# Attention over channels and a highway layer on one Trainium2 core: the instruction order from a planner with priorities replaced by a list of 1,492 tasks, and the softmax chain cut into single steps

## The chip, the cores and the metric

The kernel runs on one core of one Trainium2 chip. The metric is the device time of one execution in microseconds (us). The engines are TensorE (PE, its weight loads PEld), VectorE (DVE), ScalarE (ACT), GpSimd (POOL) and SyncE (SP). GpSimd and SyncE issue the DMA transfers here, GpSimd the loads, which turn float32 into float16 on their way, and SyncE the stores.

## What is computed

For each of four batches q, k and v have 6336 rows of 256 channels. The columns of q and k are divided by their norms over the rows, a 256 x 256 matrix of their products goes through a softmax, and v times that matrix passes through a highway layer:

```python
qn = q / (np.linalg.norm(q, axis=1, keepdims=True) + 1e-06)
kn = k / (np.linalg.norm(k, axis=1, keepdims=True) + 1e-06)
s = kn.transpose(0, 2, 1) @ qn / tau
a = np.exp(s - s.max(-1, keepdims=True))
a /= a.sum(-1, keepdims=True) + 1e-09
x = v @ a                          # for each batch, then all rows together
H = np.maximum(x @ w_h, 0.0)
T = 1.0 / (1.0 + np.exp(-(x @ w_t + b_t)))
out = T * H + (1.0 - T) * x
```

The output has 25344 rows of 256 in float32. tau is 1.

## The kernel before, in words

**Tiles.** A batch is read in six chunks of eight row blocks (128 rows by 256 channels each; a chunk of q, k or v is 1 MiB of float32) and a tail of two blocks of 96 rows. The first batch's last chunks and the second batch's first are loaded in parts. The pools hold five chunks each of q, k and v, and seven of the output (`o`).

**Stage one** (`stage1`, L440) takes the 50 row blocks of a batch one after the other and accumulates, for each half of k's channels, k'q (L452), k'k (L453) and q'q (L455) in two PSUM banks. In batches 1 to 3 the q'q matmul is left out for the first five chunks; instead ScalarE squares q (L470) and GpSimd adds the squares up (`sum_squares`, L472 to L487), and three small matmuls and copies (L516, L522) turn the sum over partitions.

**The chain** (`plan_chain`, L537) follows the last block of a batch: VectorE takes the diagonals (L569) and adds the sums (L606), GpSimd takes their square root as a power (L580), VectorE takes reciprocals (L586, L589) and spreads those of q over two diagonal matrices (L594), TensorE makes a row of them for all partitions (L628), VectorE scales the copied products (L620 copies, L634 scales), ScalarE takes exponentials (L643), TensorE transposes them (L677), the transposed blocks are copied (L533 or L535), and TensorE multiplies them by both weight matrices (L689). What results, `mr`, holds for each half of the channels the softmax itself times -0.5 (L663), and its products with w_h and w_t (L700, L702).

**Stage two** takes two row blocks of v at a time, a group; there are 25 in a batch and 100 in all, numbered g. TensorE transposes v (L760, in the last batch L754; its chunks 3 to 6 are transposed by a DMA, L768), the result is copied to SBUF (L533, L535), and three products of four matmuls follow (`products`, L800): h with the first weights, t with the second, and x (the profile calls its bank d) with the softmax. The bias is copied into the bank of t beforehand (L533, L535), or from group 67 on for odd groups added by a matmul (L831), which then uses a bank that stage one has left. ScalarE makes d from h (L840) and uu from t (L854); VectorE makes pp from both (L861) and the output o from h and pp (L880).

**What sets the order.** Every piece is a `Task` (L64) with an engine, a key (its group number plus an entry of `PRIO`, L31), two durations and what it depends on. `Plan.run` (L115) simulates the engines and the DMA queues with these numbers, at each moment picks for a free engine the ready task with the lowest key, and lets ACT or DVE take a copy, whichever is free. What comes out is the order in which the instructions are written; at run time each engine works through its own queue in that order, waiting on semaphores. Loads keep an order of their own (L421), and between the last steps of a batch's stage one and the power for k no load is issued (`loads_stop`, L615). The plan lets at most eight loads be under way.

**Stores** go out on SyncE. A store of a chunk would compete with loads; so `plan_holds` (L921) puts a small DMA before it, a hold, that reads one row of the output chunk five later (`LAG`) and so makes SyncE wait until this chunk has been begun.

Of the kernel before, what the change touches and what calls it, by code (L numbers as in the profile page):

```python
# [15 lines left out]
P = 128  # L16
# [6 lines left out]
AHEAD = 16  # L23
BY_DMA = 3
SHORT = 1.08
MOVE = 165e3
APART = 5
V_AHEAD = 2


PRIO = {  # L31
    "tr": (24.974, 16.445, 34.195, 63.304),
    "ev": (74.59, 73.008, 67.512, 50.704),
    "h": (-53.39, -86.015, -64.208, -14.641),
    "bias": (-28.394, 23.065, -1.772, 4.453),
    "t": (4.111, -1.918, 67.766, 74.312),
    "relu": (46.555, -20.175, -1.498, 14.915),
    "x": (0.958, -19.433, 43.343, -6.4),
    "gate": (-54.132, 37.28, -94.231, -112.222),
    "prod": (-40.861, -10.819, -26.763, -55.482),  # L40
    "res": (53.604, 18.42, 116.457, -9.113),
    "s1": (117.419, 42.459, 84.45),
    "sq": (-15.195, 72.384, 19.395),
}
POW = 0.75
HEAD = 5.5
TAIL = 66
EV = BIAS = ("ACT", "DVE")
ENDS = [18, 48.5, 62.25]


class Ring:


    def __init__(self, bufs):
        self.bufs = bufs
        self.freed = []

    def open_at(self, t):
        n = len(self.freed) - self.bufs  # L60
        return n < 0 or (self.freed[n] is not None and self.freed[n] <= t)


class Task:  # L64
# [3 lines left out]

    def __init__(self, eng, key, pitch, lat, deps, fn, take=(), drop=(), size=0, follows=()):
        self.eng, self.key, self.pitch, self.lat = eng, key, pitch, lat
        self.deps, self.fn, self.take, self.drop, self.size = deps, fn, take, drop, size
        self.follows = follows
        self.start = self.done = None
        self.late = 0.0
        self.soft = 0
        self.held = {}
        self.serial = False

    def engines(self):
        return self.eng if isinstance(self.eng, tuple) else (self.eng,)

    def settle(self, e):
        n = self.eng.index(e)
        self.pitch, self.lat = self.pitch[n], self.lat[n]
        self.fn = partial(self.fn, e)
        self.eng = e


class Plan:

# [8 lines left out]
    def __init__(self):  # L101
        self.tasks = []
        self.rings = {}

        self.loads_stop, self.sums_stop = [], []

    def ring(self, tag, bufs):
        self.rings[tag] = Ring(bufs)

    def add(self, *args, **kw):  # L110
        t = Task(*args, **kw)
        self.tasks.append(t)
        return t

    def run(self):  # L115
        queues = {"POOL": [], "SP": []}
        in_order = {"POOL": [], "SP": []}
        users, followers = {}, {}
        for n, x in enumerate(self.tasks):
            x.n, x.left, x.at = n, len(x.deps) + len(x.follows), 0.0  # L120
            for d in x.deps:
                users.setdefault(d, []).append(x)
            for d in x.follows:
                followers.setdefault(d, []).append(x)
            if x.size or x.serial:
                in_order[x.eng].append(x)
        for lst in in_order.values():
            lst.sort(key=lambda x: (x.key, x.n), reverse=True)
        engines = list(dict.fromkeys(x.eng for x in self.tasks if not isinstance(x.eng, tuple)))
        avail = {e: [x for x in self.tasks if e in x.engines() and not x.left and not (x.size or x.serial)] for e in engines}  # L130
        free = dict.fromkeys(engines, 2.1)
        lanes, order, events = [], [], [0.0, 2.1]
        t, left = 0.0, len(self.tasks)
        eps = 1e-6

        def ready(x):
            return (
                not x.left
                and x.at <= t + eps
                and all(self.rings[g].open_at(t + eps) for g in x.take)  # L140
                and (x.eng != "POOL" or not x.size or sum(d > t + eps for d in lanes) < self.LANES)
            )

        def finish(x, when):
            x.done = when
            events.append(when)
            for owner, tag in x.drop:
                self.rings[tag].freed[owner.held[tag]] = when
            release(users.get(x, ()), when)

        def release(us, when):
            for u in us:
                u.left -= 1
                u.at = max(u.at, when)
                if not u.left and not (u.size or u.serial):
                    for e in u.engines():
                        avail[e].append(u)

        def pick(e):
            quiet = held(self.sums_stop)  # L160
            best = min(
                (x for x in avail[e] if ready(x) and not (quiet and x.soft >= quiet)),
# [3 lines left out]
            if best is None and lst and ready(lst[-1]) and not (e == "POOL" and held(self.loads_stop)):  # L166
                return lst[-1]
# [61 lines left out]
def kernel(  # L229
# [192 lines left out]
    def natural(b):  # L422

        return b == B - 1
# [670 lines left out]
```

## Time and profile before

| | |
|---|---|
| median of three runs | 270.29 us (270.16 to 270.86) |
| span of the profiled execution | 268.3 us |
| its own time outside the span | not given; the median is 2.0 us above the span |
| TensorE, matmuls busy | 246.4 us (92%) |
| ScalarE busy | 195.1 us (73%) |
| VectorE busy | 181.6 us (68%) |
| GpSimd busy | 131.7 us (49%) |
| written by DMA | 67.24 MB |
| memory read and written | 78.38 MB and 25.95 MB |
| first matmul begins; last four matmuls (0.44 us) begin | 8.95 us; 262.04 us |

The profile is one execution seen by the hardware profiler. "Busy" is the share in which an engine had an instruction under way; ends of matmuls are modelled, so that a busy TensorE may still have short holes. A DMA share can be above 1 because packets overlap. In the slices below, each digit is one fortieth of the span (6.7 us) in tenths. A line such as `45.40:95.00 49.60, 49.09 (x488) ...` gives a stretch, its length, and the busy time and instructions of each engine in it.

### The profile page before, as it was taken

To read this page: it belongs to the slowest core of one execution; us is meant where nothing else is said; L and a number is where in the kernel's file an instruction comes from. 1 tells how busy PE (TensorE), PEld (TensorE's weight loads), DVE (VectorE), ACT (ScalarE), POOL (GpSimd) and SP (SyncE) were. 2 spreads that over 40 slices of the span, in tenths; PEclk is the share of its full clock that TensorE was granted. 3 is DMA by queue.
4 is the path that set the end of the run, shared out by engine and by line. 5 is a ranking of instruction groups with operands and counts; after the bars stand their busy time and mean duration, and the time that the engine had idled before them with its cause. 6 is when DMAs were issued, how large, how long until landed. Compare 5 with 4: busy or idle time off the path is not lost.

```text
span 268.3 us, 6249 instructions
## 1 busy us (share of the span) xinstructions
PE 246.4 (92%) x2430; PEld 216.6 (81%) x2430; DVE 181.6 (68%) x377; ACT 195.1 (73%) x365; POOL 131.7 (49%) x167
## 2 busy tenths in 40 slices
PE   0697977999999999999999999999999999999991
PEld 0596864889989978999999878999998778888880
DVE  1000035777766789557878797586878998998994
ACT  1001016978888789999898887787798999998980
POOL 7233468688778064695689138567655110000000
PEclk9999999999999999999999999999999999999998
DMA  6999999999999999999999999999999999999995
GB/s 107 215 211 208 206 206 202 212 213 214 214 213 212 213 214 255 247 263 269 275 286 258 267 267 254 249 236 281 287 280 239 284 214 304 379 399 165 351 423 232
DMA packets 24622, 67.24 MB, mean 251 GB/s; under 512 B 9104, under 2 KB 11280, under 8 KB 21648
## 3 DMA queue, kind: packets, MB, share of 16 engines
q0 software_dynamic: 13472, 39.20, 75.0%
q1 hardware_dynamic: 11120, 27.64, 29.0%
q8 instruction: 19, 0.31, 0.4%
q14 instruction: 11, 0.09, 0.1%
HBM read 78.38 MB, written 25.95 MB: 389 GB/s over the span
## 4 chain that ended last, share of the span: by engine, by line
PE 76%; DMA 12%; ACT 5%; POOL 2%; issue 2%; DVE 2%; ACTq 0%; DVEq 0%; POOLq 0%
PE h L800 16%; PE t L800 16%; PE d L800 15%; PE sg L452 12%; DMA k<-in_k_dram 10%; PE sg L453 6%; PE vtps L760 5%; DMA v<-in_v_dram 2%; ACT uu L854 2%; PE sg L455 2%; PE t L831 1%; PE vtps L754 1%; PE ah L689 1%; POOL q L327 1%; ACT d L840 1%
## 5 line engine op out<-in xcount | busy, mean ns | idle before, releaser
L800 PEld LDWEIGHTS <-vtsb 128*128 128x128 f16 (+1 forms) x1044 | 98.8, 99 | 17.3 <-issue 3.2
L452 PE MATMUL sg<-q,k 128*128 128x256 f16 x384 | 83.8, 277 | 12.7 <-DMA k<-in_k_dram 12.6
L861 DVE SCALAR_TENSOR_TENSOR pp<-uu,d 128x512 f32<-128x512 f32 (+1 forms) x100 | 68.0, 684 | 28.4 <-PE d L800 16.1
L453 PE MATMUL sg<-k 128*128 128x128 f16 x384 | 76.8, 223 | 0.0
L854 ACT ACTIVATE uu<-t 128x512 f32<-128x512 f32 (+1 forms) x100 | 59.7, 597 | 19.1 <-PE t L800 18.5
L880 DVE SCALAR_TENSOR_TENSOR o<-h,pp 128x512 f32<-128x512 f32 x96 | 65.5, 686 | 1.7
L840 ACT ACTIVATE d<-h 128x512 f32<-128x512 f32 (+1 forms) x100 | 57.9, 584 | 5.7 <-PE h L800 4.9
L800 PE MATMUL t<-mr,vtsb 128*128 128x256 f16 (+1 forms) x348 | 52.2, 272 | 1.5 <-ACT t L533 1.2
L800 PE MATMUL h<-mr,vtsb 128*128 128x256 f16 (+1 forms) x348 | 51.2, 272 | 0.5 <-ACT vtsb L533 0.5
L800 PE MATMUL d<-mr,vtsb 128*128 128x256 f16 (+1 forms) x348 | 51.5, 272 | 0.1
L452 PEld LDWEIGHTS <-k 128*128 128x128 f16 x384 | 38.0, 99 | 16.7 <-DMA k<-in_k_dram 13.9
L476 POOL TENSOR_TENSOR sq<-sq,sq 128x1024 f32<-128x1024 f32 x15 | 35.4, 2361 | 16.7 <-ACT sq L470 16.6
L453 PEld LDWEIGHTS <-k 128*128 128x128 f16 x384 | 38.0, 99 | 1.5
L533 ACT COPY t<-bias_all 128x512 f32<-128x512 f32 (+1 forms) x60 | 35.4, 591 | 1.4
L455 PE MATMUL sg<-q 128*128 128x128 f16 x144 | 32.5, 226 | 0.0
L470 ACT ACTIVATE sq<-q 128x1024 f32<-128x1024 f16 x30 | 31.3, 1053 | 0.0
L760 PE MATMUL vtps<-ident,v 128*128 128x128 f32 x144 | 27.8, 275 | 0.9 <-DMA v<-in_v_dram 0.6
L569 DVE SCALAR_TENSOR_TENSOR junk<-sg,ident 128x128 f32<-128x128 f32 x16 | 4.6, 288 | 33.2 <-PE sg L455 32.7
L535 DVE COPY vtsb<-vtps 128x256 f32<-128x256 f32 (+2 forms) x47 | 19.6, 418 | 7.0 <-PE vtps L760 6.7
L327 POOL DMA_DIRECT2D v<-in_v_dram x24 | 13.7, 571 | 18.9 <-PE vtps L760 11.7
L327 POOL DMA_DIRECT2D q<-in_q_dram x28 | 15.4, 552 | 15.1 <-DMA q<-in_q_dram 7.1
L327 POOL DMA_DIRECT2D k<-in_k_dram x28 | 15.3, 548 | 13.1 <-DMA k<-in_k_dram 9.2
(78 smaller groups left out, 249.5 us busy)
## 6 DMA issues: line engine op xcount, KB each, us to landing
out_dram<-o SPq DMA_DIRECT2D x23, 1024.0 KB, 9.6
v<-in_v_dram POOLq DMA_DIRECT2D x24, 512.0 KB, 16.6
q<-in_q_dram POOLq DMA_DIRECT2D x21, 512.0 KB, 16.2
k<-in_k_dram POOLq DMA_DIRECT2D x21, 512.0 KB, 18.0
q<-in_q_dram POOLq DMA_DIRECT2D x5, 256.0 KB, 9.6
k<-in_k_dram POOLq DMA_DIRECT2D x5, 256.0 KB, 8.9
out_dram<-o SPq DMA_DIRECT2D x2, 512.0 KB, 4.2
out_dram<-ot SPq DMA_DIRECT2D x4, 192.0 KB, 5.1
```

Of the source, the lines that this page charges most:

```text
L327: nc.gpsimd.dma_start(out=t[:, s : s + n, :], in_=main_rows(src)[:, j * CH + s : j * CH + s + n, :])
L452: nc.tensor.matmul(sg[c][:, 0:C], kc, qa, start=first, stop=False)
L453: nc.tensor.matmul(sg[c][:, C : C + P], kc, kc, start=False, stop=False)
L455: nc.tensor.matmul(sg[c][:, C + P : C + 2 * P], qa[:, cs], qa[:, cs], start=False, stop=last)
L476: add(out=sq, in0=sq, in1=other)
L533: nc.scalar.copy(out=out, in_=in_)
L760: nc.tensor.transpose(ps[:, u, 0:nr], v.bitcast(f32), ident0[0:nr, 0:nr])
L800: nc.tensor.matmul(out[0:nr, u, :], vt[u][kt][:, 0:nr], mr[kt][:, col * C : (col + 1) * C], **flags(u, kt))
L840: nc.scalar.activation(out=d[0:nr, :, :], in_=ps_t["h", b, i][0:nr, :, :], func=Act.Relu, scale=0.5)
L854: nc.scalar.activation(out=uu[0:nr, :, :], in_=ps_t.pop(("t", b, i))[0:nr, :, :], func=Act.Tanh, scale=-0.5)
L861: nc.vector.scalar_tensor_tensor(out=pp[0:nr, :, :], in0=el.pop(("uu", b, i))[0:nr, :, :], scalar=1.0, in1=ps_t.pop(("d", b, i))[0:nr, :, ...
L880: nc.vector.scalar_tensor_tensor(out=ot, in0=ps_t.pop(("h", b, i))[0:nr, :, :], scalar=0.0, in1=el.pop(("pp", b, i))[0:nr, :, :], op0=AluO ...
```

## The change

`Plan.run` no longer simulates. It walks through a list `ORDER`, written out in the file, and calls the function of each task named there; after a slash stands the engine for the copies that may run on two. `L` are loads, `s1.8` step 8 of batch 1's stage one, `tr`, `ev`, `h`, `b`, `t`, `r`, `x`, `g`, `p`, `y` with a group's number are transposes, copy, first product, bias, second product, d, third product, uu, pp and output; `sqq`, `adq`, `fsq`, `opq`, `kpq` are squares and their sums; `c1.` are steps of batch 1's chain; `O` are stores, `H` holds, `T` transposes by DMA. Keys, `PRIO`, `slot_of` and `loads_stop` are gone. A hold may now stand anywhere on SyncE's queue, and several stores may follow one hold.

In the chain each diagonal, copy and reciprocal is a task of its own. The copies of the products may go to VectorE as well. The diagonal matrices (`dcat`) are gone: the row for all partitions comes from two matmuls with the reciprocal stretched over 128 columns as weights and the identity as the moving side. The copies after the weight matrices are done in halves, 256 columns for h and 256 for t, each on ScalarE or VectorE; h products need the h halves alone, t and x products theirs. The sums of squares are kept as four blocks of 256 channels, to which each new half chunk is added, and folded at the end of the batch, where before each chunk was folded. New forms of the group's arithmetic (`FORM_B`, `FORM_D`) are in the file with empty lists and so are not used; offsets, banks and the chunks transposed by DMA are the same as before.

```diff
 LAG = 5
 UNTIL = 73
-AHEAD = 16
-BY_DMA = 3
+BY_DMA = (3, 4, 5, 6)
 SHORT = 1.08
 MOVE = 165e3
-APART = 5
-V_AHEAD = 2
...
-POW = 0.75
-HEAD = 5.5
...
+OFF = {"q": (0, 5, 5, 5), "k": (0, 0, 0, 0)}
...
 TAIL = 66
+ON_PE = tuple(g for g in range(67, 100) if g % 2)
+FORM_B = ()
+FORM_D = ()
+BANKS = {"sg0": tuple(range(68, 100, 3)), "sg1": tuple(range(67, 100, 2))}
+BUFS = {}
 EV = BIAS = ("ACT", "DVE")
-ENDS = [18, 48.5, 62.25]
-
-
-class Ring:
-
-
-    def __init__(self, bufs):
-        self.bufs = bufs
-        self.freed = []
-
-    def open_at(self, t):
-        n = len(self.freed) - self.bufs
-        return n < 0 or (self.freed[n] is not None and self.freed[n] <= t)
+SQUARES = "ACT"
+SUMS = "POOL"
+ORDER = """
...
+Lq0.0 Lk0.0 Lq0.1 Lk0.1 Lk0.2 Lq0.2 Lk0.6 Lq0.6 const Lk0.3 Lq0.3 s0.0 s0.1 s0.2 Lk0.4.0 s0.3 s0.4 s0.5 s0.6
...
+s0.43 Lw1 s0.44 Lv0.0 s0.45 s0.46 Lk1.0.4 s0.47 Lv0.1 spt c0.dq1 c0.g1/ACT ball c0.dq0 c0.dk0 c0.nq c0.g0/ACT
+c0.dk1 sqq1.0.0 s1.0 c0.nk c0.iq c0.b b0/ACT Lq1.0.4 c0.ik s1.1 spd1 Lk1.1 c0.s0 s1.2 c0.s1 Lq1.1 spd0 c0.e0
+s1.3 Lv0.2 c0.e1 c0.tr0 c0.r0 Lk1.2 c0.a0 c0.v0/ACT c0.tr1 c0.r1 c0.f0 c0.v1/ACT Lq1.2 tr0 c0.t0/DVE c0.f1
+ev0/ACT tr1 c0.h1/ACT c0.t1/DVE Lq1.3 c0.h0/DVE ev1/ACT t0 c0.a1 tr2 h0 g0 ev2/DVE h1 r0 b1/DVE tr3 x0 ev3/ACT
+r1 Lk1.3 t1 p0 tr5 x1 g1 Lv0.3 s1.4 ev5/ACT p1 b2/ACT s1.5 s1.6 y0 sqq1.0.1 tr4 t2 y1 h2 g2 s1.7 ev4/DVE r2 h3
+Lq1.4 b3/DVE tr6 adq1.0.1 r3 x2 t3 ev6/ACT p2 x3 g3 tr7 y2 b4/ACT s1.8 p3 s1.9 sqq1.1.0 Lk1.4 h4 y3 t4 r4
...
+Lv1.1 t18 y16 tr22 fsq1.1 s1.47 g18 p17 s1.48 ev22/ACT Lk2.2 sqq2.0.0 s1.49 y17 Lq2.2 h18 c1.dk0 opq1 b19/ACT
+c1.dq1 h19 c1.dk1 c1.g0/ACT r18 kpq1 t19 c1.nk c1.g1/DVE r19 tr23 c1.dq0 x18 Lv1.2 ev23/DVE g19 s2.0 p18 s2.1
+b20/ACT tr25 x19 y18 ev25/ACT Lv1.6 s2.2 sqq2.0.1 c1.rq tr26 Lk2.3 p19 t20 s2.3 c1.nq ev26/DVE g20 h20 y19
+tr27 adq2.0.1 r20 s2.4 b21/DVE h21 sqq2.1.0 c1.iq x20 ev27/DVE t21 r21 p20 s2.5 g21 tr24 x21 y20 adq2.1.0
+ev24/ACT s2.6 b22/ACT p21 tr28 h22 ev28/DVE t22 r22 y21 c1.b g22 c1.ik x22 Lv1.3 h23 b23/ACT c1.s1 Lq2.4 c1.s0
+s2.7 p22 t23 c1.e0 s2.8 r23 c1.r0 s2.9 c1.e1 y22 c1.tr0 x23 g23 c1.r1 c1.tr1 s2.10 c1.v1/ACT p23 s2.11
...
+c1.a0 r24 s2.13 b25/DVE h25 sqq2.1.1 x24 c1.a1 t25 r25 p24 adq2.1.1 s2.14 g25 s2.15 ev30/DVE x25 y24 b26/ACT
+tr31 s2.16 p25 sqq2.2.0 h26 ev31/DVE t26 y25 r26 adq2.2.0 s2.17 s2.18 g26 H6 x26 b27/ACT O0.0.0 tr32 h27 p26
+ev32/ACT O0.2.0 t27 r27 y26 O0.1.0 tr33 s2.19 g27 x27 ev33/DVE sqq2.2.1 b28/DVE h28 tr34 p27 t28 r28 adq2.2.1
...
+s2.20 ev34/DVE g28 x28 y27 sqq2.3.0 tr35 b29/DVE s2.21 h29 p28 t29 r29 Lk2.4 ev35/DVE s2.22 g29 y28 s2.23
...
+p36 tr44 r37 t37 y36 s2.36 g37 s2.37 x37 b38/ACT h39 p37 t38 r39 ev44/DVE s2.38 g38 s2.39 y37 s2.40 b39/ACT H9
+h38 t39 H5 r38 tr45 O0.6 x39 g39 ev45/DVE x38 O0.3.0 b40/ACT p39 tr46 H7 s2.41 sqq2.4.1 ev46/DVE t40 O0.4.0
+y39 s2.42 g40 adq2.4.1 p38 h40 tr47 b41/ACT y38 s2.43 r40 t41 ev47/DVE s2.44 g41 x40 Lk3.2 tr48 b42/DVE h41
+Lq3.1 ev48/ACT p40 s2.45 Lk3.1 r41 t42 y40 Lv2.1 x41 g42 fsq2.0 tr49 h42 ev49/DVE b43/ACT s2.46 p41 r42 tr50
...
+c2.s0 s3.4 p45 c2.e0 t46 c2.s1 s3.5 c2.r0 c2.e1 s3.6 y44 c2.tr0 g46 s3.7 c2.tr1 c2.v0/DVE s3.8 b47/ACT y45
...
+y52 s3.23 ev59/ACT x53 g54 h54 b55/ACT p53 s3.24 r54 tr60 t55 y53 sqq3.2.1 x54 ev60/DVE h55 p54 g55 adq3.2.1
...
+h58 p57 t58 r58 tr62 y57 Lv2.5 s3.35 g58 x58 adq3.4.0 ev62/DVE b59/ACT s3.36 p58 tr63 t59 ev63/ACT h59 y58 g59
+s3.37 r59 tr64 H14 b60/DVE h60 Lq3.6 ev64/ACT H8 x59 r60 Lv2.6 tr66 O1.2.0 t60 p59 H10 s3.38 ev66/DVE g60 x60
+O1.3.0 y59 tr65 b61/ACT s3.39 O1.5.0 p60 h61 ev65/ACT O1.6 t61 r61 O1.4.0 tr67 g61 s3.40 ev67/DVE s3.41 y60
+b62/ACT x61 sqq3.4.1 H13 t62 p61 tr68 s3.42 g62 adq3.4.1 y61 s3.43 h62 ev68/DVE h63 b63/DVE r62 s3.44 r63 t63
+Lv3.0 tr69 x62 g63 Lv3.6 s3.45 b64/ACT p62 fsq3.0 x63 s3.46 p63 t64 Lv3.1 y62 s3.47 g64 fsq3.1 s3.48 y63 H15
...
+h77 g77 tr81 p76 h78 r77 t78 ev81/DVE r78 y76 x77 T3.3 g78 tr82 x78 p77 ev82/ACT h79 b80/DVE t79 r79 p78 t80
+g79 y77 x79 g80 tr83 y78 h80 ev83/ACT b82/DVE t81 O3.0.0 r80 p79 tr84 h81 g81 x80 y79 r81 T3.5 t82 p80 h82
+ev84/DVE x81 r82 y80 t83 g82 p81 h83 b84/ACT tr85 y81 x82 r83 H16 t84 ev85/ACT H17 p82 h84 g83 T3.4 x83 y82
...
+h93 O3.1.0 x92 y91 r93 t94 g93 p92 x93 g94 h94 y92 t95 r94 p93 h95 b96/ACT x94 y93 g95 t96 r95 p94 h96 g96 x95
+y94 r96 t97 p95 b98/ACT O3.4.0 h97 x96 y95 r97 t98 g97 p96 h98 x97 y96 r98 g98 p97 x98 O3.5.0 h99 p98 t99 r99
+y97 x99 g99 y98 p99 O3.5.4 y99 O3.6
+"""
...
     def run(self):
+        done = {id(x) for x in self.tasks.values() if x.fn is None}
+        for token in ORDER.split():
+            name, _, e = token.partition("/")
+            x = self.tasks[name]
+            assert all(id(d) in done for d in [*x.deps, *x.follows]), name
+            x.fn(e) if e else x.fn()
+            done.add(id(x))
+        assert len(done) == len(self.tasks)
...
+    def squares(nm, b, j, n, e):
+        x = tiles[(nm, b, j)][:, n * H : (n + 1) * H, :]
+        if j == n == 0:
+            out = acc_t[nm, b] = small.tile([P, H, C], f32, tag=f"acc_{nm}", name=f"acc_{nm}{b}")
         else:
-            sq = sq_t.pop((b, j, 0))
-            if j == 0:
-                sums[b] = small.tile([P, C], f32, tag="sums", name=f"sums{b}")
-                add(out=sums[b], in0=sq[:, 0, :], in1=sq[:, 1, :])
-            else:
-                add(out=sq[:, 0, :], in0=sq[:, 0, :], in1=sq[:, 1, :])
-                add(out=sums[b], in0=sums[b], in1=sq[:, 0, :])
+            out = sq_t[nm, b, j, n] = new("sq", [P, H, C], f32, f"sq_{nm}{b}_{j}_{n}")
+        if e == "ACT":
+            nc.scalar.activation(out=out, in_=x, func=Act.Square)
+        else:
+            (nc.vector if e == "DVE" else nc.gpsimd).tensor_tensor(out=out, in0=x, in1=x, op=AluOp.mult)
+
+    def add_square(nm, b, j, n, e):
+        eng, acc = nc.gpsimd if e == "POOL" else nc.vector, acc_t[nm, b]
+        eng.tensor_tensor(out=acc, in0=acc, in1=sq_t.pop((nm, b, j, n)), op=AluOp.add)
+
+    def fold_sums(nm, b, n, e):
+        eng, acc = nc.gpsimd if e == "POOL" else nc.vector, acc_t[nm, b]
+        if n == 0:
+            eng.tensor_tensor(out=acc[:, 0:2, :], in0=acc[:, 0:2, :], in1=acc[:, 2:4, :], op=AluOp.add)
+        else:
+            sums[nm, b] = s = small.tile([P, C], f32, tag=f"sums_{nm}", name=f"sums_{nm}{b}")
+            eng.tensor_tensor(out=s, in0=acc[:, 0, :], in1=acc[:, 1, :], op=AluOp.add)
...
-        dq = dve(
-            lambda: (diagonal(0), diagonal(1), rest_of_q()), 0.9, 0.95, [last, consts] + sums_of_q
-        )
-        nq = pool(lambda: norm(0), POW, POW + 0.2, [dq])
-        dk = dve(lambda: (diagonal(2), diagonal(3)), 0.75, 0.8, [dq])
-        nk = pool(lambda: norm(2), POW, POW + 0.2, [dk])
-        stop = plan.tasks[plan.tasks.index(last) - 3]
-        plan.loads_stop.append((stop, nk))
...
+        ends = {}
+        for nm in "qk":
+            n = 0 if nm == "q" else 2
+            x = [add(f"d{nm}{c}", "DVE", 0.36, 0.42, [last, consts], partial(diagonal, n + c)) for c in range(2)]
+            if nm in kept:
+                x = [add(f"r{nm}", "DVE", 0.2, 0.25, x + [kept[nm]], partial(rest, nm))]
+            x = add(f"n{nm}", "POOL", 0.75, 0.8, x, partial(norm, n))
+            ends[nm] = add(f"i{nm}", "DVE", 0.4, 0.45, [x], partial(recip, n))
+
+        def copy_g(c, e):
+            if "gs" not in st:
+                st["gs"] = small.tile([P, 2, C], f32, tag="gs", name=f"gs{b}")
+            copy(e, st["gs"][:, c, :], sg_t[b][c][:, 0:C])
+
+        gs = [
+            add(
+                f"g{c}", ("ACT", "DVE"), (0.3, 0.35), (0.42, 0.45), [last], partial(copy_g, c),
+            )
+            for c in range(2)
+        ]
+        for c in range(2):
+            users = [plan.tasks[f"c{b}.{n}"] for n in (f"dq{c}", f"dk{c}", f"g{c}")]
+            add(f"j{c}", "NONE", 0, 0, users, None, drop=[own[c]])
+
+        def bcast():
+            st["cqb"] = new("vt", [P, 2, P], f32, f"cqb{b}")
             for c in range(2):
...
+        def evac_ah(c, n, e):
+            o = rows_of(c)[:, (n + 1) * C : (n + 2) * C]
+            a, r = st["ah", c][:, n * C : (n + 1) * C], st["ri"][:, c : c + 1]
...
     def plan_holds():
-        for x, b, j in chunk_stores:
+        for z, b, j, own in chunk_stores:
             n = b * NJ + j + LAG
-            y, g = begun.get(n, (None, 1e9))
-            if g > UNTIL:
-                x.key = max(x.key, UNTIL + 1.6)
-                continue
-            x.key = g + 1.6
-            plan.add(
-                "SP", g + 1.5, 0.1, 0, [y], lambda n=n: hold(n // NJ, n % NJ), size=1024,
-            )
+            if n in begun and begun[n][1] <= UNTIL and f"H{n}" not in plan.tasks:
+                y = begun[n][0]
+                plan.add(
+                    f"H{n}", "SP", 0.1, 0, [y], lambda n=n: hold(n // NJ, n % NJ), size=1024,
+                )
+        for n in range(B * NJ):
+            own = [x for x in chunk_stores if x[1] * NJ + x[2] == n]
+            ends = [x[0] for x in own] + [x for x in [plan.tasks.get(f"H{n}")] if x]
+            plan.add(f"jo{n}", "NONE", 0, 0, ends, None, drop=[(own[0][3], "o")])
 
 
     ready = {}
```

## The prediction

> **What bounds the kernel now.** I read the slices first, then a table of stretches, then the chain that ended last, then the waits of TensorE, and last the queue of the stores.
>
> ```profile
> PE   0697977999999999999999999999999999999991
> DMA  6999999999999999999999999999999999999995
> GB/s 107 215 211 208 206 206 202 212 213 214 214 213 212 213 214 255 247 263 269 275 286 258 267 267 254 249 236 281 287 280 239 284 214 304 379 399 165 351 423 232
> ```
>
> TensorE is full from the eighth slice on, and the DMA engines are full from the second. Two resources bound this kernel together. GB/s counts what was written: a load writes two bytes for four read, so 213 GB/s is 426 GB/s of float32, or 2.46 us for each MiB of input.
>
> ```profile
> 8.95:36.70 27.75, 25.98 (x303) 23.12 (x303) 0.00 (x0) 1.17 (x2) 10.41 (x19) 1.00 1.10 209
> 36.70:45.40 8.70, 5.74 (x47) 3.80 (x45) 6.13 (x25) 4.24 (x10) 6.73 (x11) 1.00 1.15 200
> 45.40:95.00 49.60, 49.09 (x488) 43.84 (x489) 34.65 (x61) 41.92 (x75) 33.73 (x38) 1.00 1.07 213
> ...
> 150.00:156.00 6.00, 5.07 (x52) 4.35 (x49) 4.85 (x22) 5.14 (x12) 2.28 (x4) 1.00 1.06 268
> 156.00:204.00 48.00, 48.00 (x490) 43.47 (x488) 36.68 (x69) 38.82 (x72) 30.90 (x32) 1.00 1.06 261
> ```
>
> The columns are the stretch, its length, and busy time of TensorE, weight loads, VectorE, ScalarE and GpSimd, then clock, DMA share and rate. TensorE starts at 8.95 us. Up to 45.40 us it idles 1.77 + 2.96 us; afterwards only the turns of a batch show idle time, 0.93 us in the one from 150 to 156 us.
>
> ```profile
> 37.52 0.88 POOL inv L580 x2
> 38.40 0.48 issue
> 38.88 5.76 DMA v<-in_v_dram
> 44.64 0.14 issue
> 44.77 0.43 PE vtps L760 x2
> 45.20 0.02 issue
> 45.22 0.38 ACT vtsb L533
> 45.60 0.05 issue
> 45.65 0.61 PE h L800 x4
> ```
>
> The first value tile is queued on GpSimd behind the two powers of the first softmax chain, lands at 44.64 us and only then lets the first product start, at 45.65 us.
>
> ```profile
> PE t L800 <- ACT t L533: 1.2, 3, 0.7
> PE vtps L760 <- ACT vtsb L533: 0.3, 1, 0.3
> PE d L800 <- ACT d L840: 0.3, 1, 0.3
> PE t L800 <- ACT d L840: 0.2, 1, 0.2
> ```
>
> These are all of TensorE's waits between 48 and 263 us: 2.0 us, none of them for a DMA.
>
> ```profile
> 100.35 0.62 SPq L919 DMA_DIRECT2D held_row<-o  x1
> 101.04 0.67 SPq L894 DMA_DIRECT2D out_dram<-o  x1
> ```
>
> The first store is issued at 101.04 us and lands 9.5 us later; the next five single stores took 11.2, 10.2, 7.9, 9.2 and 9.5 us.
>
> **What the Trainium skill says.** "DMA: Bandwidth & Descriptors", section "Issuing engines are not separate DMA queues", says that transfers from all issuing engines run on the same 16 DMA engines and interleave. The trace agrees: while the first store moved (105 to 109.5 us) its 1 MiB took some 4.5 to 5 us, and from 156 to 204 us the 261 GB/s, with four chunk stores and a tail store in it (4.4 MB), mean 8.1 MB of f16 loads, thus 16.3 + 4.4 = 20.7 MB in 48 us, 430 GB/s: mixing costs nothing and gains nothing. "TensorE: Matmul & The Clock Gate", Part 1, says that the array runs at half clock by default and after idle windows. The trace shows it at the start only: matmul triples of stage one are 0.43 us apart up to 13.6 us, later 0.22 us. After the hole at 36.7 us (1.6 us) they are at full pace.
>
> **The change, part by part.** The profiled span is 268.3 us; the median is 270.29 us, so 2.0 us lie around the span, and I add them at the end.
>
> Work: I count instructions by pitch on TensorE. 300 products of four matmuls at 0.437 us (0.44 in the chain) make 131.1. Stage one: 80 steps with three matmuls a half at 0.443 and 120 with two at 0.333 make 75.4. 87 pairs of transposes at 0.22 make 19.1, 17 bias matmuls at 0.218 make 3.7, four chains at 2.2 make 8.8, sums and presets 1.6. Total 239.7 us, the same after the change: the same offsets, banks and transposes by DMA, only spelt differently. The broadcast becomes two f32 matmuls of 128 columns in place of one of 256, equal columns, 0 us; it reads a stretched column as weights, which no row shows, and I bound that at 0 to 0.3 us a chain and take 0. VectorE loses 8 scalings of 0.28 us (1.9 us, not the bound) and shares the copies of the Gram blocks. On GpSimd a batch's sums cost 9 x 2.36 + 1.28 + 0.73 = 23.2 us for 24.8 before. Bytes, loads, holds and stores are the same.
>
> Head: v0.0 and v0.1 are now issued ahead of the powers. v0.0 ends at 14.88 MiB of loads: 5 us (start and landing, fitted to the last tile of batch 0: 12.38 MiB at 35.8 us) + 14.88 x 2.46 = 41.6 us in place of 44.64. So the chain is late next. Before, its last copies (mr, two of 0.75 us) end at 44.93 us. The scalings take 0.48 us off it, and copies of half width on two engines some 0.75 us; the first product then starts at about 43.8 us, 1.85 us earlier. But the order gives TensorE only four steps of batch 1 in that hole where eight were done: 4 x 0.333 = 1.33 us come back later. Net gain 0.5 us (0 to 1.2). q1.0 and k1.0 are late next, and s1.4 waits for them at 46.5 us.
>
> Turns and steady stages: in 45.40 to 262.5 us, 217.1 us, 239.7 - 27.9 = 211.8 us of work were done, so 5.3 us are lost, more than the idle time shows, since short holes vanish in pipelined ends. The three single-column sums (some 0.4 us each) stay. Chains are now cut into single steps among the pieces of stage two, so that copies of the bias (the 1.2 us above) need not wait behind them. I would take 2 to 2.5 us of it if nothing else bound.
>
> DMA: this is what caps it. I add up the order's bytes before each step of stage one, and TensorE's work before it. s1.8 needs 18.88 MiB, 5 + 46.4 = 51.4 us; TensorE is there at 43.8 + (34.7 - 27.4) = 51.1. s3.8: 56.01 + 6.19 of stores = 62.2 MiB, 158 us, against 43.8 + 112.5 + 2 of losses = 158.3. s3.24: 61.01 + 9.19 = 70.2 MiB, 177.7 us, against 43.8 + 131.0 + 2 = 176.8: there the DMA comes last, by about 1 us. From it 239.7 - 158.4 = 81.3 us of work remain, with 1.3 us of losses at the last turn: TensorE ends at 260.3 us for 262.5, net of the whole 2.2 us. Loads that come earlier than this would have to take bytes from the stores; these are as full.
>
> Stores: the holds change. Before, a hold waits for the chunk five later, and a ring of seven tiles leaves eight groups, about 17 us, for landing. Now the first, H6, waits for y25, and y29 needs the tile of O0.0.0: 9.3 us of TensorE's work, less 0.7 of y25 and 0.55 of the hold: 8.05 us. Landing alone took 7.9 to 11.2. I cost it at nothing, because the order issues no load between 82.8 and 99.4 us of TensorE's work: 44.82 MiB are through at 5 + 110.3 = 115.3 us, and the store, issued at about 112 us, moves its first bytes 3.9 us later (101.04 to 105 before), at 115.9 us, alone: 2.5 us for 4.9, landing after some 7.5 us. If that cover is gone, VectorE stands still in y29 with every later product behind it.
>
> End: the last five VectorE steps and a store of 192 KB follow TensorE's end as before: 5.8 us. Ahead of the last transpose, T3.4, the DMA engines have 92.1 MiB and three transposes, for which I allow 7 us (an estimate from the 8 us of low rates after 240 us): 5 + 226.6 + 7 = 238.6 us; T3.4 and 7.4 MiB are 21 us more, 260 us, within TensorE's tail. Sum: 260.3 + 5.8 = 266.1 us, + 2.0 = 268.1 us.
>
> **The rivals.** (a) All holes close: the head gives 1.2 us and the stages 4 of their 5.3, as DMA rate is 430 rather than 426 GB/s and loads are ahead: 270.3 - 5.2 = 265.1 us. For it: no DMA wait after 48 us now; against: the DMA slices. (b) No change: the DMA engines, full in every slice, end when they did, since the transposes beside a pile of stores waste as much (240 to 250 us shows rates near 50 GB/s), or a gain in the head is lost at s1.8 and s3.24 by 1 us each more: 270.0 us. (c) Slower: the stores land too late for the ring. If loads are still queued when O0.0.0 starts, it lands after 9.5 to 11.2 us, 1.5 to 3.1 us late for y29, and O0.1.0, third in line at 4.9 us each, after 19.3 us for 16 us: 3.3 us late in all; the same happens with O0.3.0 at y41 (8.5 us of room, behind a tail store): 2 us. 268.1 + 5.3 = 273.4 us. It decides from a load queue some 2 us later than my 115.3 us.
>
> **How the numbers follow.** Forecast 268.1 us, chance 0.42 (its own range 266.8 to 269.4); (a) 265.1, 0.16; (b) 270.0, 0.17; (c) 273.4, 0.25. About 0.3% (0.8 us) is what a measurement of this kernel can tell from no change. Faster is forecast and (a): 0.58; same (b): 0.17; slower (c): 0.25. The range, 264.5 to 272.5, takes in (a) and (b) and the smaller half of (c), whose stall can be anything from 1.5 us; that leaves out some 0.05 below and 0.15 above.
>
> **What would show it.** Right: first h product at 43.5 to 44.2 us; TensorE's waits after 48 us with some DMA k or q, below 2 us; last d product near 260 us. Wrong: VectorE's result waiting for DMA out_dram for over 1 us around 120 to 130 us (c), a first product still after 45 us, or GpSimd's powers of a later chain stuck behind a load.

## The result, and the profile after

The changed kernel takes 280.94 us (median of four runs, 280.03 to 283.07) beside 270.23 us for the kernel before: a ratio of 1.040 [1.036, 1.045]. It is slower by 10.7 us, where I had forecast 2.2 us less; the time lies outside my range. Of all runs here one is left out of its kernel's median, because it fell into a slow state of the chip (281.92 us, of the kernel without H16 and H17); two of the expectations below take it in and say 277.6 us for 277.1.

The profiled run of the changed kernel is the longest of its four (its span 281.3 us, the others 278.3, 278.3 and 280.0). Its slices, to be read against those of the kernel before:

```profile
PE   0797978999999999999995799999999999994991
...
PEclk9999999999999999999999589999999999999898
DMA  6999999999999999999979997999899999995995
GB/s 114 214 212 207 199 199 214 212 215 214 210 211 214 214 212 211 329 299 209 214 139 289 271 213 269 294 216 213 146 387 258 234 187 388 284 268 133 404 421 220
```

TensorE, which was full to the end before, now has two dents: the slices 22 and 23 (from 148 us) and slice 37 (from 253 us). The granted clock sinks to 5 tenths behind the first. The DMA slices dip to 7 tenths just ahead of the first (slice 21) and to 5 in the second. The table of stretches, made at these places (same columns as in the prediction), shows what happens in them:

```profile
149.00:155.50 6.50, 2.21 (x26) 1.91 (x25) 0.41 (x2) 2.23 (x4) 1.04 (x2) 0.85 1.04 303
155.50:165.00 9.50, 8.74 (x50) 6.79 (x50) 6.25 (x21) 3.81 (x8) 2.50 (x4) 0.56 1.06 249
...
256.00:260.00 4.00, 0.31 (x3) 0.02 (x2) 1.57 (x3) 0.88 (x2) 0.00 (x0) 0.92 0.92 221
260.00:263.00 3.00, 3.00 (x16) 2.17 (x17) 0.17 (x1) 1.09 (x2) 0.00 (x0) 0.54 0.98 355
```

Each hole is followed by a stretch at about half clock (0.56 and 0.54), in which TensorE counts as busy and does half as much: 50 matmuls in 9.5 us. TensorE's waits name the two holes; in the kernel before, none of its waits after 48 us was for a DMA:

```profile
PE h L726 <- DVE o L859: 4.9, 1, 4.9
PE t L726 <- DMA vT<-v: 3.7, 1, 3.7
```

The first wait is for VectorE, but VectorE's own step (`o`, L859) had itself waited for an output store:

```profile
DVE o L859 <- DMA out_dram<-o: 6.1, 1, 6.1
```

The chain that ended last shows what that store had waited for:

```profile
139.38 4.78 DMA held_row<-o
144.16 0.02 issue
144.18 0.50 SPq L903
144.68 0.04 issue
144.72 0.75 SPq L871
145.47 0.05 issue
145.51 9.72 DMA out_dram<-o
```

L903 is a hold. H9 was issued at 139.38 us, and H5, next in the queue, could be issued only when H9 had landed, 4.78 us later. Every hold writes the same tile, `held_row`, so each one is a write after a write. Behind H5 stood the tail store O0.6 (L871) and then O0.3.0, which was issued at 145.51 us and landed 9.72 us later. The output y41 needs the tile of that store back before it can be written.

The second hole, in the same view:

```profile
246.53 5.02 SPq L694
251.55 0.04 issue
251.59 3.41 DMA held_row<-o
255.01 0.02 issue
255.02 0.50 SPq L903
...
255.62 4.31 DMA vT<-v
```

Again two holds in a row: H16 lands after 3.41 us, only then does H17 go out, and T3.4 (L694), the transpose that TensorE needs next, stands behind both. SyncE's waits sum this up (us in total, times, longest); the second line is that of the kernel before:

```profile
SPq L903 <- DMA held_row<-o: 36.0, 8, 11.3
SPq L919 <- DMA held_row<-o: 35.4, 9, 5.7
```

That line of the kernel before could be had when I made the forecast. I did not read it.

What the two holes cost in this execution can be estimated by counting matmuls. With H5 left out (below), TensorE does 159 matmuls between 149 and 165 us, against 76 here: 83 x 16.0/159 = 8.4 us. With H16 and H17 left out it does 110 in the 12 us from 252 us, 9.2 a microsecond, so 64 in 7 us against 3 + 16 = 19 here: 45 / 9.2 = 4.9 us. Together 13.3 us; the profiled spans differ by 281.3 - 268.3 = 13.0 us. That the two figures agree so closely is in part chance: with H5, H16 and H17 all left out (below), 4.6 of the 10.7 us remain. And the price of a hole differs from one execution to the next: in the profile of the kernel without H16 and H17 the first hole is a wait of 4.4 us and TensorE does 104 matmuls from 149 to 165 us, about 5.5 us lost by the same reckoning, with 3.4 us at half clock instead of 10.2.

### The profile page after: what moved, and what is told of

Its sections match the earlier page's. It is cut to its first block, busy times and chain, and to the rows that moved or that the text cites. A ratio compares the mean times of both kernels' runs of the same rounds, so it can differ in the third digit from the quotient of the medians.

```text
span 281.3 us, 6255 instructions
## 1 busy us (share of the span) xinstructions
PE 250.1 (89%) x2438; PEld 220.0 (78%) x2438; DVE 187.4 (67%) x375; ACT 195.5 (69%) x367; POOL 127.6 (45%) x143
## 4 chain that ended last, share of the span: by engine, by line
PE 62%; DMA 22%; DVE 9%; SPq 3%; issue 2%; ACT 1%; POOL 1%; DVEq 0%; POOLq 0%
PE t L726 13%; PE d L726 12%; PE h L726 12%; PE sg L368 10%; DMA q<-in_q_dram 6%; DMA k<-in_k_dram 6%; PE sg L370 5%; PE vtps L686 5%; DMA out_dram<-o 3%; DMA held_row<-o 3%; DMA v<-in_v_dram 2%; DVE pp L813 2%; DVE o L859 2%; SPq L694 2%; DMA vT<-v 2%
## 5 line engine op out<-in xcount | busy, mean ns | idle before, releaser
L726 PEld LDWEIGHTS <-vtsb 128*128 128x128 f16 (+1 forms) x1044 | 99.8, 100 | 19.8 <-issue 7.3
L368 PE MATMUL sg<-q,k 128*128 128x256 f16 x384 | 85.6, 278 | 13.3 <-DMA k<-in_k_dram 10.9
L399 POOL TENSOR_TENSOR acc_q<-acc_q,sq_q 128x1024 f32<-128x1024 f32 x27 | 63.9, 2368 | 43.4 <-ACT sq_q L393 42.9
L370 PE MATMUL sg<-k 128*128 128x128 f16 x384 | 78.0, 223 | 0.0
L859 DVE SCALAR_TENSOR_TENSOR o<-h,pp 128x512 f32<-128x512 f32 x96 | 65.6, 687 | 8.1 <-DMA out_dram<-o 6.1
L726 PE MATMUL h<-mr,vtsb 128*128 128x256 f16 (+1 forms) x348 | 52.6, 276 | 5.0 <-DVE o L859 4.9
L726 PE MATMUL d<-mr,vtsb 128*128 128x256 f16 (+1 forms) x348 | 52.7, 276 | 0.0
L477 ACT COPY t<-bias_all 128x512 f32<-128x512 f32 (+1 forms) x55 | 32.6, 593 | 1.1
L393 ACT ACTIVATE sq_q<-q 128x1024 f32<-128x1024 f16 x27 | 28.5, 1057 | 0.0
L477 ACT COPY gs<-sg 128x256 f32<-128x256 f32 x7 | 2.6, 375 | 35.8 <-DVE junk L494 35.8
L479 DVE COPY t<-bias_all 128x512 f32<-128x512 f32 x28 | 19.4, 692 | 6.4 <-ACT uu L802 6.1
## 6 DMA issues: line engine op xcount, KB each, us to landing
v<-in_v_dram POOLq DMA_DIRECT2D x24, 512.0 KB, 13.3
k<-in_k_dram POOLq DMA_DIRECT2D x5, 256.0 KB, 12.6
```

The source lines that it names most:

```text
L368: nc.tensor.matmul(sg[c][:, 0:C], kc, qa, start=first, stop=False)
L370: nc.tensor.matmul(sg[c][:, C : C + P], kc, kc, start=False, stop=False)
L399: eng.tensor_tensor(out=acc, in0=acc, in1=sq_t.pop((nm, b, j, n)), op=AluOp.add)
L477: nc.scalar.copy(out=out, in_=in_)
L726: nc.tensor.matmul(out[0:nr, u, :], vt[u][kt][:, 0:nr], mr[kt][:, col * C : (col + 1) * C], **flags(u, kt))
L859: nc.vector.scalar_tensor_tensor(out=ot, in0=ps_t.pop(("h", b, i))[0:nr, :, :], scalar=0.0, in1=el.pop(("pp", b, i))[0:nr, :, :], op0=AluO ...
```

## The experiments

Theory A: holds wait for each other's landing because they share one row, and what is queued behind them on SyncE (stores with waiting readers, transposes) is late. Theory B: the room of the output ring, four groups after the hold, is too short by itself, whatever the holds do. The edits are to the changed kernel if nothing else is said. What a hold writes is never read, so leaving holds out or moving them changes no output.

**A row for each hold.** No wait is edited; its cause goes.

```diff
-    held_row = const.tile([1, C], f32, tag="held_row")
+    held_row = const.tile([1, 13, C], f32, tag="held_row")
-        nc.sync.dma_start(out=held_row, in_=og[(b, j)][0:1, 0, :])
+        nc.sync.dma_start(out=held_row[:, b * NJ + j - LAG, :], in_=og[(b, j)][0:1, 0, :])
```

> Each hold writes a row of its own instead of the one shared row; nothing else changes. Theory A (a hold waits for the landing of the hold before it, so that two or three in line make the next store or transpose late): both holes of TensorE go, the one before y41 (4.3 us idle and some 4.2 us of half clock) and the one before the products of chunk 3.4 (3.7 and 1.3 us); 280.9 - 13.5 = 267 to 269 us. Theory B (the ring of seven output tiles leaves four groups, which is too short for a store that runs beside loads, 9.7 us from issue to landing): O0.3.0 goes out 4.3 us earlier but y41 still waits some 2 us with half clock after it; 272 to 276 us.

Measured: 272.04 us, 1.0076 [1.0057, 1.0095] of the kernel before. SyncE's queue at the first hole, with start and length of each group:

```profile
139.77 1.14 SPq L903 DMA_DIRECT2D held_row<-o  x2
140.95 0.58 SPq L871 DMA_DIRECT2D out_dram<-ot  x1
141.57 0.43 SPq L873 DMA_DIRECT2D out_dram<-o  x1
```

The two holds take 1.14 us, which is the 0.55 us each of my prediction, and O0.3.0 leaves at 141.57 instead of 145.51 us, 3.94 us earlier. VectorE waits for no store in the whole run, and of TensorE's waits this is the largest after 48 us:

```profile
PE t L726 <- DMA vT<-v: 1.5, 1, 1.5
```

So the shared row makes 8.9 of the 10.7 us. Theory B falls, though only just at this place: with the same ring, margins and places of the stores, O0.3.0 lands 8.0 us after 141.57 us, and VectorE writes y41 from 149.65 us, less than 0.1 us later.

**Single holds left out.** H5 alone; and H16 with H17:

```diff
+SKIP = ('H5',)            # the other kernel: ('H16', 'H17')
...
+            if name in SKIP:
+                continue
```

> The hold H5 alone is left out (it stands behind H9 and ahead of O0.6 and O0.3.0). Theory A: the first hole goes and the second stays, 280.9 - 8.5 = 272 us. Theory B: y41 still waits about 2 us, 276 to 278 us.

> The holds H16 and H17 alone are left out (they stand ahead of the transpose T3.4). Theory A: the first hole stays and the second goes, 280.9 - 5 = 276 us. If the transpose is late for another cause (SyncE blocked by the transposes before it, or the DMA engines being full of stores), the second hole stays and the time is 280 to 281 us.

Measured: 277.01 us, 1.022 [1.015, 1.029], and 277.11 us (three runs), 1.026 [1.020, 1.031]. Each edit takes away its own hole. Without H5, at the first hole:

```profile
149.00:155.50 6.50, 6.50 (x72) 6.02 (x71) 5.80 (x19) 5.84 (x12) 3.38 (x6) 1.00 1.03 280
155.50:165.00 9.50, 8.93 (x87) 7.65 (x85) 7.93 (x22) 7.33 (x17) 4.09 (x5) 1.00 1.06 214
```

Without H16 and H17, at the second:

```profile
252.00:258.00 6.00, 6.00 (x55) 5.08 (x53) 5.66 (x9) 5.48 (x12) 0.00 (x0) 1.00 1.07 327
258.00:264.00 6.00, 6.00 (x55) 5.20 (x54) 5.66 (x10) 5.56 (x12) 0.00 (x0) 1.00 1.01 420
```

But the gains, 3.9 and 3.8 us between medians, are smaller than what the holes cost in the profiled execution (8.4 and 4.9 us), which is the longest of its four and 2.1 us above the median. There is a second reason. Without H5, TensorE comes to the last transposes earlier and waits longer there:

```profile
PE t L729 <- DMA vT<-v: 5.3, 1, 5.3
```

That is 5.3 us where the changed kernel waits 3.7. T3.4 leaves at 250.75 us for 255.62, 4.9 us earlier, while TensorE had gained some 8 us at the first hole: T3.4 still stands behind H16 and H17 in SyncE's queue.

**Three holds left out together,** H5, H16 and H17:

> The changed kernel with three of its thirteen holds left out, H5, H16 and H17, and nothing else; the row is still shared by the other ten. Leaving out H5 alone gave 277.0 us and H16 with H17 alone 277.6, 3.9 and 3.3 less than the changed kernel, while all holds on rows of their own gave 272.0, 8.9 less. If the two holes of TensorE are the whole loss and each is made by the holds named, then the two edits together give what the own rows give, 271.5 to 273 us, more than the sum of the two (273.7), since each hole left alone takes back part of what the other gives. If the other ten holds cost by themselves (they too wait for each other on the shared row), the time stays near the sum or above it, 273.7 to 275.

Measured: 274.85 us, 1.017 [1.013, 1.020]: not 272, so sharing the row among the other ten holds costs 2.8 us as well. (The sum of the two gains, with 277.1 for the second kernel, gives 273.2 us; the measured time lies above it.) SyncE's queue shows a third place:

```profile
204.36 19.13 SPq L906 DMA_DIRECT2D held_row<-o  x3
223.54 1.51 SPq L697 DMA_TRANSPOSE vT_t<-v_t  x1
225.11 3.38 SPq L876 DMA_DIRECT2D out_dram<-o  x4
```

Three holds stand in SyncE for 19 us; the tail transpose and four stores leave behind them at 223.54 to 228 us. With own rows the same three holds take 8.3 us, since one of them still waits for its chunk to be begun, and the tail transpose leaves at 211.08 us. All that follows on SyncE is late, and TensorE waits for `vT` twice, 2.7 us in all.

**The half clock by itself.** Is it the idle time that costs, or the slow clock behind it? Twenty matmuls, whose result nothing reads, are put ahead of h43, where the hole is, with the copy ev51 moved ahead of them:

```diff
-b44/DVE tr51 c2.g0/ACT h43 y42 ev51/ACT
+b44/DVE tr51 c2.g0/ACT ev51/ACT fill h43 y42
...
+        junk = new("vt", [P, 2, C], f32, "fill")
+        for _ in range(20):
+            nc.tensor.matmul(junk, row0, btb, start=True, stop=True)
```

> Twenty matmuls of 512 columns whose product nobody reads are put into the first hole, ahead of h43; the wait of y41 stays as it is. If the half clock after the hole costs its 4.2 us: the records show full clock from 156 to 165 us and the time is 277 us. If the pieces after the hole are limited by ScalarE and VectorE anyway, it stays at 280 to 281 us.

Measured: 280.4 us, 1.036 [1.030, 1.041], which is not told apart from the changed kernel. The clock is held:

```profile
149.00:155.50 6.50, 6.04 (x46) 3.82 (x44) 2.31 (x5) 2.33 (x5) 1.24 (x2) 1.00 1.00 228
155.50:165.00 9.50, 9.50 (x93) 8.33 (x90) 6.83 (x25) 7.08 (x17) 2.50 (x4) 1.00 1.05 244
```

Of 139 matmuls up to 165 us 20 are filling; the other 119 are 43 more than in the changed kernel, about 4.3 us of work. The medians (280.4 and 280.9 us) don't show it. The two profiled executions do in part; but one is the shortest of its four and the other the longest. T3.4 leaves 3.9 us earlier (251.74 us for 255.62), and the last four matmuls begin 2.6 us earlier: behind the second hole TensorE stays at half clock for 6.8 us, for 3.4 in the changed kernel. Also, the filling is longer than the hole:

```profile
151.95 4.48 PE L901 MATMUL fill<-btb,row 128*128 128x512 f16 x20 [0.46 <-ACT vtsb L477]
153.61 0.69 DVE L859 SCALAR_TENSOR_TENSOR o<-h,pp 128x512 f32<-128x512 f32 x1 [4.09 <-DMA out_dram<-o]
```

y41 is done at 154.30 us, and h43, which waited for it in the changed kernel, begins only at 156.26, behind the filling, which so delays it by 2.0 us itself. This run settles little. I gave the filling to the kernel without H16 and H17 too, which has no second hole:

> H16 and H17 left out and the twenty unread matmuls in the first hole, so that the second hole can't take back what the fill gives. If the half clock after a hole costs what the records show (9.5 us at a clock of 0.56), 277.6 - 4 = 273.6 us. If that work is limited by other engines anyway, 277 to 278 us.

Measured: 278.95 us, 1.031 [1.028, 1.034]; without the filling it was 277.1. Up to 165 us TensorE has done 118 matmuls besides the filling, 14 more than the 104 without it, but it now waits for the transposes:

```profile
PE t L729 <- DMA vT<-v: 3.3, 2, 2.1
```

SyncE comes to T3.3 at 232.61 us, 1.5 us later than without the filling (231.07), behind the same three holds. So the work won in the middle gained nothing here: the transposes are dated by SyncE's queue. What the half clock costs by itself neither run tells cleanly.

**The rest of 1.8 us.** With own rows, one wait of 1.5 us for `vT` was left: T3.5 is queued ahead of T3.4, and its value tile comes late (GpSimd's load of v3.5 waits 19.2 us for T3.3 to free its buffer). T3.4 ahead of T3.5, which is the order of use:

```diff
-... r81 T3.5 t82 ... h84 g83 T3.4 x83 ...
+... r81 T3.4 t82 ... h84 g83 T3.5 x83 ...
```

> Own rows for the holds, and the transposes T3.4 and T3.5 change places on SyncE's queue. In the run with own rows alone T3.4 stood behind T3.5, which waited for v3.5, and TensorE then waited 1.5 us for T3.4 while the DMA engines idled at a share of 0.53 from 240 to 246 us. If that order is what is left: the hole goes, the stores at the end start some 3 us earlier, and the time is 269 to 270 us, level with the kernel before. If the transposes are late because the DMA engines are behind, it stays at 272 us.

Measured: 272.04 us, 1.0061 [1.0039, 1.0083]. The wait is gone and the time is not better. The same swap with one row and eight holds left out (H5, H7, H8, H10, H12, H13, H16, H17):

> Eight holds (H5, H7, H8, H10, H12, H13, H16, H17) are left out, five stay (H6, H9, H11, H14, H15), and T3.4 and T3.5 change places. If the holds that are left out did nothing but cost time, it equals the run with own rows and the swap, 269 to 270 us. If they were needed to keep stores from the loads' way, loads come late and it is 271 to 274 us.

Measured: 271.90 us, 1.0057 [1.0039, 1.0074]. In this profile TensorE has no hole, and its last four matmuls begin 0.75 us earlier than before (first line: before):

```profile
262.04 0.60 PE L800 MATMUL d<-mr,vT_t 128*96 128x256 f16 x4 [0.29 <-ACT d L840]
261.29 0.60 PE L729 MATMUL d<-mr,vT_t 128*96 128x256 f16 x4
```

(Theory C below says that TensorE is done at 260.3 us; I had taken the last product on the chain for its last one.) Yet the kernel is 1.6 us slower. What is later is the last store. SyncE's queue there:

```profile
234.35 12.07 SPq L697 DMA_TRANSPOSE vT<-v  x2
246.48 1.21 SPq L876 DMA_DIRECT2D out_dram<-o  x1
247.75 0.42 SPq L874 DMA_DIRECT2D out_dram<-ot  x1
248.27 14.28 SPq L876 DMA_DIRECT2D out_dram<-o  x7
```

T3.5 holds SyncE until its load has landed. Three stores whose outputs were done long before (O2.5.0, O2.6, O2.4.0) stand behind it, while the DMA engines have this to do (in the kernel before, a share of 1.12 and 198 GB/s in the same stretch):

```profile
240.00:246.00 6.00, 6.00 (x55) 5.19 (x53) 5.66 (x10) 5.64 (x13) 0.00 (x0) 1.00 0.61 111
```

What was not stored then has to be stored later. The last store's time from issue to landing is the last column of its row; before:

```profile
out_dram<-ot SPq DMA_DIRECT2D x1, 192.0 KB, 2.7
```

and with the eight holds left out and the swap:

```profile
out_dram<-ot SPq DMA_DIRECT2D x1, 192.0 KB, 5.5
```

The last store is issued at 263.53 us (before: 264.60) and needs 2.8 us longer. So the three stores go ahead of T3.5, in both kernels:

```diff
-... T3.4 t82 ... g83 T3.5 x83 ... g86 O2.5.0 x85 ... t87 O2.6 p85 ... g89 O2.4.0 x88
+... T3.4 O2.4.0 O2.5.0 O2.6 t82 ... g83 T3.5 x83 ... g86 x85 ... t87 p85 ... g89 x88
```

> The changed kernel without the holds H5, H7, H8, H10, H12, H13, H16 and H17, with T3.4 ahead of T3.5, and now with the stores O2.4.0, O2.5.0 and O2.6 right behind T3.4, ahead of T3.5, which moves to g83. The question is the rest of 1.6 us over the kernel before that was left once both holes of TensorE were gone (271.9 us). Theory C: TensorE is done at 260.3 us there, earlier than before, and the end is set by stores: SyncE stands 12 us at T3.5, which waits for the load v3.5, while three outputs that are ready (2.2 MB, 5.3 us at 420 GB/s) stand behind it and the DMA engines move 160 to 200 GB/s. With them ahead, the DMA engines are full in 234 to 246 us, about 2 us less is left after TensorE, and the time is 268.5 to 270. Theory D: the stores delay the load v3.5 and T3.4 by as much as they take, so the idle time of the DMA engines only moves; then TensorE waits for vT, 1 us or more, and the time is 271.5 or more.

> As the run beside it, but with all holds kept, each on a row of its own: the changed kernel with its own plan of holds, the row no longer shared, T3.4 ahead of T3.5, and O2.4.0, O2.5.0 and O2.6 ahead of T3.5. Theory C (the stores stand behind T3.5's wait for its load): 268.5 to 270 us, and no hole of TensorE over 2 us. Theory D (the stores only trade places with the transposes): 271.5 or more, as without the move (272.0). If the holds on rows of their own cost something still, this is over the run without them by up to 1 us.

Measured: 270.81 us, 1.0017 [0.9999, 1.0036], and 270.94 us, 1.0024 [1.0008, 1.0041]. Both are 0.8 to 0.9 us above theory C's range and 0.6 to 0.7 below theory D's: 1.1 us is won in each, TensorE waits for `vT` for 0.3 and 0.4 us only, and the stretch that was half empty moves twice as much:

```profile
240.00:246.00 6.00, 6.00 (x55) 5.18 (x54) 5.67 (x10) 5.64 (x12) 0.00 (x0) 1.00 1.05 254
```

That is the first of the two kernels. Its last store lands after 4.5 us instead of 5.5, but leaves 1.0 us later; this profiled execution is 1.1 us above its median and doesn't show the gain. In the second kernel the last store lands after 4.1 us, for 7.4 with own rows and the swap alone (a profile that is the longest of its six). Three small edits thus take the changed kernel to 0.2% above the kernel before (0.1 to 0.4% with own rows). With own rows for all holds it is not distinguishable from eight holds fewer: what a hold costs is the wait for the one ahead of it.

**Two edits to the kernel before.** A row of its own for each hold:

> The kernel before with one edit: each of its holds writes a row of its own instead of the one they share. In its profile SyncE waits 35.4 us in 9 waits for an earlier hold to land, as long as in the changed kernel. If these waits cost where stores with waiting readers stand behind them (theory A), then the kernel before, in which no product waits for an output store, gains little: 269.5 to 270.3 us, no change within 0.3%. If the shared row delays stores everywhere by itself, it gains 1 us or more: 269.2 or less. If the waits for the row are what keeps the stores out of the loads' way, as a hold is meant to do, it gets slower: 271 or more.

Measured: 270.29 us, 1.0005 [0.9995, 1.0016]. In its profile no wait for `held_row` is left, and the time is the same. The 35 us in which SyncE waited for holds cost the kernel before nothing; no engine waits for an output store in its profile.

And the one step of the head alone, v0.0 issued ahead of the powers:

```diff
-    for x in plan.run():
+    order = plan.run()
+    v0 = ld["v", 0, 0][0]
+    order.remove(v0)
+    order.insert(order.index(powers[0]), v0)
+    for x in order:
```

> The kernel before with one instruction moved: the load of the first value tile is issued ahead of the powers of the first chain. My step on the head: the chain is late next at 44.9 us, the first product starts some 0.6 us earlier, 269.7 to 270.0 us. If the DMA engines cap the later steps (each MiB at 2.46 us), nothing of it reaches the end: 270.2 us. If the power is held up behind the load's lane, 270.5 to 271 us.

Measured: 269.73 us, 0.9973 [0.9957, 0.9988], the fastest of all kernels here and within what I expected. Yet its profile does not show the gain where I had placed it:

```profile
35.80 8.78 DMA v<-in_v_dram
```

The load leaves 3.1 us earlier and lands at 44.58 us, 0.06 us before the old time: the DMA share was 1.16 meanwhile, and the first product starts at 45.59 us, for 45.65. So the number came true without its mechanism. This profiled execution is the longest of its ten and no shorter than the profiled one of the kernel before (270.10 and 270.16 us), so it can't show where the 0.6 us come from.

## Why the prediction was wrong, step by step

- **The step that failed** is the term for the stores, "I cost it at nothing", with its hold of 0.55 us. It priced the issue of one hold and asked whether the store behind it lands in time. It left out that a hold following another is issued only when that one has landed: 4.78 us for H9 (H5 behind it), 3.41 us for H16 (H17 behind it), and 18.4 us in SyncE for three holds at 209 us (8.3 with own rows). In place of nothing this term measured 8.9 us, the difference that a row for each hold makes. The measured time is 12.8 us above the forecast (280.9 - 268.1); the three stores behind T3.5 are 1.1 us more of that, and 2.8 us stay open. "The Trainium skill", page "DMA: Bandwidth & Descriptors", section "Two DMAs through the same engine are not ordered", says of a transfer that reads what an earlier one writes that the issuing engine has to wait for the earlier one's semaphore. Here two transfers write the same row, and the trace shows the same kind of wait, 36.0 us in 8. The new order puts holds in pairs, and stores and transposes that are needed soon right behind them. With a row for each hold the 0.55 us are right (1.14 for two).
- **The cover named for y29 held.** O0.0.0 left at 113.90 us and landed 6.7 us later; no step waited for it. I worked the margin out where the order was safe, and named y41 without working it out.
- **Rival (c)** had the sign and one of the places, y41, with 2 us; the first part, 3.3 us at y29, did not come. At y41 the wait was 6.1 us. The store left 3.94 us later than with own rows, and then took 9.72 us to land, for 8.0; four loads had been issued from 145.25 to 146.86 us, at the time it left. (c) looked for slow landings and not for a late start, so its sign was in part luck. Its price also lacked the half clock behind a hole, with which a wait of 4.9 us cost about 8.4 in the profiled execution.
- **The end.** "Ahead of the last transpose ... T3.4 and 7.4 MiB are 21 us more" summed bytes. T3.4's date came from SyncE's queue, not from bytes: it left at 255.62 us, behind H16 and H17, while the DMA share was at 0.09 (255 to 257 us).
- **TensorE's end** was forecast 2.2 us earlier, 260.3 for 262.5 us. With the eight holds left out and the swap, so without holes, it is 261.29 + 0.44 = 261.7 us: 0.8 of the 2.2 us are there. Where the other 1.4 us went no run here tells. And "within TensorE's tail" was wrong: I let the DMA engines end at 260 us and carried the tail of 5.8 us over unchanged. With the stores that T3.5 keeps back, the last one takes 5.5 us to land for 2.7, and the span goes on for 8.4 us after TensorE (270.1 - 261.7).
- **The head** was half right: v0.0 landed at 42.88 us (41.6 forecast, 44.64 before), the first product of the chain at 44.16 us (43.8 forecast), but it was followed by a wait for the second copy until 44.94 us, and the first h product came at about 45.5 us, nearly as before (45.65).

## What to carry to other kernels

Before you cost an entry of an in-order queue at its issue time, read what that queue waits for: a row like `SPq L903 <- DMA held_row<-o` means that each entry costs a landing, and whether that hurts depends only on what stands behind it. When an order is rewritten, go through each queue for pairs of that kind and for stores that are ready and stand behind a transfer that is not. And a hole that is closed in the middle pays only if the queue that dates the next transfer moves too: without H5 the kernel got back 3.9 us of a hole that cost about 8.4 in the profiled execution.

## What the runs showed of the hardware

The Trainium skill's "TensorE: Matmul & The Clock Gate", Part 1, says that an idle window of some 3.4 us brings the array to half clock and that about 3.4 us of sustained work ends it. The first agrees roughly: behind both holes, of 4.9 and 3.7 us, the clock falls to 0.50. But it falls 2.3 and 3.1 us after the last matmul has ended, and in two other profiles after 2.0 us (last hole of the filled kernel) and 4.1 us (first hole without H16 and H17). The second differs. Two-microsecond stretches of the changed kernel:

```profile
154.00:156.00 2.00, 0.00 (x0) 0.00 (x0) 0.67 (x2) 0.00 (x0) 0.00 (x0) 0.50 1.04 309
...
162.00:164.00 2.00, 2.00 (x14) 1.57 (x12) 1.19 (x5) 0.13 (x1) 0.85 (x2) 0.55 1.07 215
164.00:166.00 2.00, 2.00 (x21) 1.84 (x20) 0.71 (x5) 1.77 (x4) 0.00 (x0) 1.00 1.05 211
```

TensorE restarts at 156.07 us and is at full clock only from 163.8 us, 7.7 us later; after the second hole it took 2.8 us. Read in stretches of 0.1 us, the half clock lasts 10.24 us behind the first hole and 3.41 us behind the second; in the two other profiles it lasts 6.83 us (filled kernel) and 3.41 us (without H16 and H17). These are three, one, two and one times 3.41 us. In these traces, then, the clock is raised only some whole number of such steps after it fell, and that number decides much of what a hole costs. Why it was three behind the first hole no run here tells.

A 1 KB transfer inside the chip, a hold, landed after anything from 1.6 to 12.6 us (median 3.4) in this kernel and after 4.1 to 6.9 us (median 5.0) in the kernel before. Its size doesn't explain that, and the load on the DMA engines not alone: H16 landed 3.41 us after 251.59 us, while the DMA share was 0.01 from 253 to 256 us.
